# First expert of the first 448-column chunk in three passes; weights split by single parts in the experts' order; tokens split behind the ring

## The chip, the cores and the metric

The kernel runs on one core of a Trainium2 chip. The metric is device time in microseconds (us), less is better. The engines named below are TensorE (PE, with its weight loads as PEld), VectorE (DVE), ScalarE (ACT), GpSimd (POOL) and SyncE (SP, whose instruction stream issues most of the DMAs).

## The reference

Two stages run one after the other. The first is a linear attention with a polynomial sketch (4 batches, 4 heads, 1088 positions, head size 32, sketch size 8):

```python
a = einsum('rd,bhsd->bhsr', S1, x); b = einsum('rd,bhsd->bhsr', S2, x)   # for x = q and x = k
phi = outer product of a and b along r, 64 features
kv = sum over s of phi(k) v;  z = sum over s of phi(k)
out = (phi(q) kv) / (phi(q) z + 1e-6)
```

Its result, laid out as x[4352, 128], goes through four experts (E = 4, F = 1024) whose results are weighted with the normalised `domain_probs`:

```python
for e in range(4):
    h = maximum(x @ w1[e], 0)            # 4352 x 1024
    out += p[:, e:e+1] * (h @ w2[e])     # 4352 x 128
```

Everything is in float32.

## The kernel before

**Chunks and steps.** The 4352 tokens are cut into chunks of `CHUNKS = [128, 448, 512] + [448] * 7 + [128]` columns, numbered m = 0 to 10. In a chunk, each expert has eight tiles of 128 hidden rows, numbered k, and a step is two tiles. A chunk has NQ = 16 steps, four for each expert, so steps 0 to 15 are chunk 0, steps 16 to 31 chunk 1 (16 to 19 its expert 0, 20 to 23 expert 1, 24 to 27 expert 2, 28 to 31 expert 3), and step 32 opens chunk 2. A step stands in the program as half-steps, one for each tile. The program's order on each engine is fixed by the Python loop at the end; no engine reorders.

**Forms of a product.** Chunks 0 and 10 are "plain": products in float32 on half-width weights (L236). In the other chunks a first-layer tile is made in one of two ways. The float32 way is one product (`first`, L1111) and one Relu on ACT (L1113). The three-pass way (L1119 to L1129) works on numbers split into parts, tagged a, b and d, in the faster fp32r type: two products (L1124 with xa and wa, L1125 with xb and wb), a rescaling of the PSUM tile in place on ACT (L1126), a third product (L1173 with xd and wd) that is issued behind the next tile's first two, and then ACT's Relu: L1181 where the tile goes whole into the second layer, or L1176, followed by DVE's L1150 and L1153, where the hidden tile itself is split into ha, hb, hd. Before the change, expert 0 of chunk 1 takes the float32 way and all other experts of chunks 1 to 9 take three passes:

```python
def three_first(m, e):
    return not plain(m) and not (m == 1 and e == 0)
```

**The second layer.** In chunk 1 the experts 0 and 1 multiply whole hidden tiles in float32 (L1222). From expert 2 of chunk 1 on, six of an expert's eight tiles go through three passes in the order of `DEAL`, and the tiles 2 and 7 whole (all L1241). When an expert is finished, `gather` brings its PSUM bank out (`ev`, L1270 on ACT for a whole expert, L1244 on ACT and L1273 on DVE else), and POOL multiplies it with the gate and adds it to the chunk's total (L1280, L1282).

**The splits.** All weights and tokens are split on the fly, `split` on ACT (L896) and `join` on DVE (L899). A first-layer weight of an expert has six parts: a on ACT, b and d on DVE, for each half of its 1024 columns. The second-layer weights (`second_weight_parts`, two calls for an expert) take ACT 128x768, DVE 128x256 and 128x512 in the first call, and the same again in the second; the second ACT operation overwrites what the first pair of DVE joins reads, so it waits for them. `token_parts` makes xa on ACT, xb and then xd on DVE. The table `to_part` says behind which step each call stands: first-layer weights of the experts 1, 2, 3 and 0 from the steps 12, 13, 16 and 19 on, second-layer weights of the experts 2, 3, 0, 1 from the steps 16, 19, 22, 32 on, the tokens of chunk 1 behind the steps 17 and 18.

**Work beside it.** The attention of later tokens is cut into pieces (`plan`, `piece`, `work`) that are issued between the tiles: transposes kT (L387) and qT (L570), key projections (L430) with their ACT copies (L433) and DVE sums (L440), the copies of v into `vx` (`value_copy`, L396, L401), query projections (L236 from qT and sx, L761, then DMAs to `qd` and back), products (L782) and more. The columns of chunk 1 are written into the tile `ring` by small copies on DVE, POOL and ACT (L712) at about step 12. `gate_rows`, `store_gates` and `load_gates` compute and spread the gates by way of L330 on DVE, L331 on POOL, a transpose `pt` on DVE (L338) and DMAs of SP and POOL.

PSUM has six banks for tiles tagged h, which the first-layer tiles share with the pieces, and one each for o0 and o1.

Of the kernel before, what the change touches and what calls it, by code (L numbers as in the profile page):

```python
# [17 lines left out]
def _ap(t, p0: int, np_: int, off: int, free):  # L18

    p = list(t.ap)[0]  # L20
    return bass.AP(t.tensor, t.offset + p0 * p[0] + off, [[p[0], np_]] + [list(d) for d in free])
# [3 lines left out]
def kernel(  # L25
# [24 lines left out]
    nc = tc.nc  # L50
# [3 lines left out]
    B, H, S, D = q.shape  # L54
    E, DM, F = w1.shape
# [6 lines left out]
    NQ = E * FB // 2  # L62
# [13 lines left out]
        a6=10, b6=10, d5=11, d6=11, x7=11,  # L76
    )
    UNITS = [[P, 448, 512], [448, 448, 192], [256, 448, 384], [512, 320, 256]]

    CHUNKS = [P, 448, 512] + [448] * 7 + [P]  # L80
    NC = len(CHUNKS)
# [44 lines left out]
    kn, qn, vn = {}, {}, {}  # L126
# [10 lines left out]
    w1_of, w2_of = {}, {}  # L137
# [254 lines left out]
            nc.vector.transpose(kT[:, 1024:S], kn[b][:, 1024:S])  # L392

    def value_copy(b):
        for r in range(2):
            nc.scalar.copy(  # L396
                vx[:, 4 * r : 4 * r + 4, :, 0:D].rearrange("p t h d -> p h t d"),
                _ap(vn[b], 0, P, P * r, [[8 * D, H], [D, 4], [1, D]]),
            )
            yield  # L400
        nc.scalar.copy(vx[0:64, 8, :, 0:D], _ap(vn[b], 0, 64, 1024, [[D, H], [1, D]]))  # L401

    def key_project(b, gi, kf):

# [453 lines left out]
    def queries(b, c, n):  # L858
        qc = early.pop((b, c))
        qf = apool.tile([P, QW], F32, tag="qf", name="qf")  # L860
        nc.vector.stream_shuffle(in_=qc[:, 0:n], out=qf[:, 0:n], mask=mask_lo)
        yield
        nc.vector.tensor_tensor(out=qf[:, 0:n], in0=qc[:, 0:n], in1=qf[:, 0:n], op=ALU.add)
        free()
        yield
        qb = apool.tile([P, QW], F32, tag="qb", name="qb")
        nc.vector.stream_shuffle(in_=qf[:, 0:n], out=qb[:, 0:n], mask=mask_b)
        yield
        qp = query_tiles()
        for x in range(2):  # L870
            qa = apool.tile([P, QW], F32, tag="qa", name="qa")
            nc.vector.stream_shuffle(in_=qf[:, 0:n], out=qa[:, 0:n], mask=mask_a[x])  # L872
            yield
            for p in range(2):
                query_product(qp, p, x, n, qa, qb)
                yield
        yield
        yield
        yield
        yield from attend(b, c, n, qp)  # L880
# [10 lines left out]
    wa = cpool.tile([P, E, F], F32R, name="wa")  # L891
# [3 lines left out]
    def split(a, w, scale):  # L895
        nc.scalar.activation(a, w, ACTF.Copy, scale=scale * NEAR)  # L896

    def join(out, in0, scale, in1, op):
        nc.vector.scalar_tensor_tensor(out=out, in0=in0, scalar=scale, in1=in1, op0=ALU.mult, op1=op)  # L899

    def weight_parts(e):

        HF = F // 2
        for c in (slice(0, HF), slice(HF, F)):
            w, a, b, d = (x[:, c] for x in (w1_of[e], wa[:, e], wb[:, e], wd[:, e]))
            split(a, w, 4096.0)
            join(b, w, -4096.0, a.bitcast(F32), ALU.add)
            yield
            join(d, a.bitcast(F32), -R12, b.bitcast(F32), ALU.subtract)
            yield  # L910

    w2_parts = {}

    def second_weight_parts(e):


        w, n = w2_of[e, 0], N3 * DM
        vab = cpool.tile([P, F], F32R, tag=f"w1_{e}", name="vab")  # L920
        vb = cpool.tile([P, 2 * n - F], F32R, tag=f"vb_{e}", name="vb")
        a, lows = vab[:, 0:n], [(0, F - n, vab[:, n:F]), (F - n, n, vb[:, :])]
        split(a, w, 4096.0)
        for c, z, b in lows:
            join(b, w[:, c:z], 4096.0, a[:, c:z].bitcast(F32), ALU.subtract)
        yield
        split(a, w, 1.0)
        d = cpool.tile([P, n], F32R, tag=f"w2_{e}0", name="vd")[:, :]
        for c, z, b in lows:
            join(d[:, c:z], b.bitcast(F32), 1.0, a[:, c:z].bitcast(F32), ALU.subtract)  # L930
        w2_parts[e] = [
            tuple(x[:, DM * i - c : DM * i - c + DM] for x, c in ((a, 0), next((x, c) for c, z, x in lows if DM * i < z), (d, 0)))
            for i in range(N3)
        ]
        yield
# [114 lines left out]
    def plain(m):  # L1050
        return m in (0, NC - 1)
# [2 lines left out]
        return m == 1 and e < E // 2  # L1054

    def three_first(m, e):
        return not plain(m) and not (m == 1 and e == 0)

    begun_hp, made_hp = {}, {}

# [203 lines left out]
    def gather(m, e):  # L1264

        n = CHUNKS[m]
        o0, o1 = acc.pop((m, e))
        if o0 is None:
            ev = mpool.tile([P, CW], F32, tag="ev", bufs=1, name="ev")
            nc.scalar.copy(ev[:, 0:n], o1[:, 0:n])  # L1270
        else:
            ev = evs.pop((m, e))
            nc.vector.tensor_tensor(out=ev[:, 0:n], in0=ev[:, 0:n], in1=o1[:, 0:n], op=ALU.add)  # L1273
        g = gate.pop((m, e))[:, 0:n]
        if e == 0:
            total[m] = mpool.tile([P, CW], F32, tag="total", bufs=1, name="total")
        for c in range(0, n, 256):
            x = slice(c, min(c + 256, n))
            to = total[m] if e == 0 else ev
            nc.gpsimd.tensor_tensor(out=to[:, x], in0=ev[:, x], in1=g[:, x], op=ALU.mult)  # L1280
            if e:
                nc.gpsimd.tensor_tensor(out=total[m][:, x], in0=total[m][:, x], in1=ev[:, x], op=ALU.add)  # L1282
        yield
        later = m + (e + 2) // E
        if not plain(later):
            load_gates(later, [(e + 2) % E])
        if e == E - 1:
            yield
            yield

            for _ in range(0 if m + 2 < NC else 4):
                yield
            turn_back(m, total.pop(m)[:, 0:n])
# [40 lines left out]
        begun_hp[i] = psum(ps_h, "h")  # L1334
        half_columns(i, begun_hp[i], 0)
    to_part = {}
    for e, at, then in zip((1, 2, 3, 0), (12, 13, 16, 19), (32, 16, 19, 22)):
        for at, parts_of in ((at, weight_parts(e)), (then, second_weight_parts(e))):
            for step in range(at, at + 4):
                to_part.setdefault(step, []).append(parts_of)  # L1340
    for m in range(1, NC - 1):
        at, tokens = NQ * m - 4 if m > 1 else NQ + 1, token_parts(m)
        for step in (at, at + 1):
            to_part.setdefault(step, []).append(tokens)
    ending = iter(())

    def close(m, e):
# [40 lines left out]
    for i in range(len(steps) + LA):  # L1388
        if i < len(steps):
            m, kq = steps[i]  # L1390
            until_there(START[m] + CHUNKS[m])
            rate = max(
                [0]
                + [
                    (needed[c] - spent[0]) / max(sum(rooms[2 * i : 2 * NQ * c - (EARLY if c > 1 else 13)]), 0.3)
                    for c in range(m + 1, NC)
                    if 2 * NQ * c - (EARLY if c > 1 else 13) > 2 * i
                ]
            )

            def work():

                now[0] += 1
                if not NQ <= i < NQ + 2:
                    credit[0] = min(credit[0] + rate * rooms[min(now[0], len(rooms) - 1)], 0.5)
                if holds[0]:
                    credit[0] = max(credit[0], 0.01)
                while credit[0] > 0:
                    cost = piece()
                    credit[0] -= cost  # L1410
                    if not cost:
                        break

            first(i, work, lambda j: behind(2 * i + j))
            to_due(i)
            if kq == NQ - 4 and 0 < m < NC - 2:
                until_there(START[m + 1] + CHUNKS[m + 1])
            for parts_of in to_part.get(i, ()):
                next(parts_of, None)
            if i == 2:  # L1420
                gate_quotients()
            elif i == 8:
                later_weights()
            elif i == 5:
                load_batch(1)
            elif i == 12:
                gate_rows()
            elif i == 13:
                later_mask()
                store_gates(range(1))  # L1430
                load_gates(1, range(2))
            elif 14 <= i < 14 + B - 1:
                store_gates(range(i - 13, i - 12))
            if m == NC - 2 and kq == NQ // 2:
                until_there(B * S)
                load_last()
        if i == LA:

            made_hp[3] = psum(ps_h, "h")
            for c in (0, HP):  # L1440
                half_columns(3, made_hp[3], c)
        if NQ * (NC - 1) <= i < NQ * (NC - 1) + 2:
            continue
        if not behind(2 * i + 1):
            next(ending, None)
# [29 lines left out]
```

## Time and profile before

| | |
|---|---|
| median of 3 runs | 451.4 us (451.22 to 453.52) |
| the profiled execution's own time | 451.43 us |
| its span | 449.6 us, so 1.83 us lie around it |
| granted TensorE clock | 1.00 in all stretches that were looked at |
| PE, DVE, ACT, POOL busy | 443.5, 359.0, 330.6, 120.0 us |

Chunk 0 multiplies from about 14 to 33 us, and the eight float32 tiles of chunk 1's expert 0 start at 28.43 us. Chunk 2's first tile starts at 76.34 us. The busy time of PE includes waits inside its pipeline, because the ends of matmuls are modelled. The distance from the start of one matmul to the start of the next one that is not itself waiting is a better measure of what a matmul costs. A number in square brackets behind a row is idle time of that engine ahead of it, with what ended it.

### The profile page before, as it was taken

The numbers are of one execution on the slowest core, as the hardware profiler recorded it, in microseconds if no ns is written. First come the engines' busy times: TensorE is split into PE (matmuls) and PEld (weight loads), VectorE is DVE, ScalarE is ACT, GpSimd is POOL, SyncE is SP. The second block draws the span as 40 slices with busy tenths as digits, with TensorE's granted clock in tenths as the row PEclk, the third lists the DMA queues.
The fourth block names the chain that finished last, engine by engine and source line by source line (L and its number), as shares of the span: only waits on it lengthen the run. The fifth ranks groups of instructions, "written<-read, shape, count | busy, mean of one in ns | idle before, by whom it ended". The sixth has DMA issues, their size and how long they took to land.

```text
span 449.6 us, 8655 instructions
## 1 busy us (share of the span) xinstructions
PE 443.5 (99%) x3013; PEld 367.4 (82%) x3013; DVE 359.0 (80%) x606; ACT 330.6 (74%) x699; POOL 120.0 (27%) x206
## 2 busy tenths in 40 slices
PE   8999999999999999999999999999999999999997
PEld 5875678777778888888888888888888888888886
DVE  5887779887988896889879869787779787787753
ACT  4268888677867876778687767787788788877741
POOL 7352133210323132212322312134123212321320
PEclk9999999999999999999999999999999999999999
DMA  7964641014223403242252142410321121117401
GB/s 200 298 143 142 189 129 49 26 33 124 94 55 91 120 23 80 52 128 68 68 127 24 22 117 72 123 47 21 95 53 30 30 46 40 22 37 219 154 2 28
DMA packets 53779, 38.45 MB, mean 86 GB/s; under 512 B 26920, under 2 KB 49896, under 8 KB 53736
## 3 DMA queue, kind: packets, MB, share of 16 engines
q1 hardware_dynamic: 53064, 37.77, 31.9%
q8 instruction: 23, 0.38, 0.3%
q0 software_dynamic: 448, 0.07, 0.2%
q14 instruction: 20, 0.16, 0.1%
q10 hardware_dynamic: 224, 0.07, 0.1%
HBM read 32.68 MB, written 5.21 MB: 84 GB/s over the span
## 4 chain that ended last, share of the span: by engine, by line
PE 94%; DVE 3%; DMA 1%; ACT 1%; issue 0%; SPq 0%; DVEq 0%
PE o L1241 40%; PE h L1173 13%; PE h L1124 13%; PE h L1125 13%; PE h L236 7%; PE o L236 3%; PE o L1222 2%; PE h L1111 1%; PE h L430 1%; DMA kn<-in_k_dram 1%; DVE qp L583 1%; DMA vn<-in_v_dram 0%; ACT h L1126 0%; DVE qa L872 0%; DVE rd L615 0%
## 5 line engine op out<-in xcount | busy, mean ns | idle before, releaser
L1126 ACT ACTIVATE h<-h 128x448 f32<-128x448 f32 (+1 forms) x280 | 151.3, 540 | 74.0 <-PE h L1125 69.5
L1150 DVE SCALAR_TENSOR_TENSOR hb<-h,ha 128x448 fp32r<-128x448 f32 (+1 forms) x204 | 125.9, 624 | 54.5 <-ACT ha L1176 53.2
L1124 PE MATMUL h<-xa,wa 128*128 128x448 f32 (+1 forms) x280 | 130.3, 465 | 0.0
L1153 DVE SCALAR_TENSOR_TENSOR hd<-ha,hb 128x896 fp32r<-128x896 f32 (+1 forms) x102 | 116.7, 1144 | 8.2
L1176 ACT ACTIVATE ha<-h 128x448 fp32r<-128x448 f32 (+1 forms) x204 | 111.7, 548 | 0.0
L1173 PE MATMUL h<-xd,wd 128*128 128x448 f32 (+1 forms) x280 | 103.5, 370 | 0.5 <-ACT h L1126 0.4
L1125 PE MATMUL h<-xb,wb 128*128 128x448 f32 (+1 forms) x280 | 103.1, 368 | 0.0
L1280 POOL TENSOR_TENSOR ev<-ev,gate 128x256 f32<-128x256 f32 (+1 forms) x54 | 40.9, 757 | 219.4 <-DVE ev L1273 201.7
L1241 PE MATMUL o<-ha,vab 128*128 128x448 f32 (+1 forms) x204 | 76.3, 374 | 0.0
L1125 PEld LDWEIGHTS h<-xb,wb 128*128 128x128 f32 x280 | 52.7, 188 | 18.8 <-issue 14.8
L1124 PEld LDWEIGHTS h<-xa,wa 128*128 128x128 f32 x280 | 52.7, 188 | 18.7 <-issue 13.5
L1241 PE MATMUL o<-hid,w_sb 128*128 128x448 f32 (+1 forms) x136 | 62.9, 544 | 0.0
L1173 PEld LDWEIGHTS h<-xd,wd 128*128 128x128 f32 x280 | 52.5, 187 | 9.2 <-ACT h L1126 2.6
L1241 PE MATMUL o<-hd,vd 128*128 128x448 f32 (+1 forms) x204 | 58.9, 370 | 0.0
L1241 PE MATMUL o<-hb,vb 128*128 128x448 f32 (+1 forms) x136 | 49.9, 368 | 0.0
L1282 POOL TENSOR_TENSOR total<-total,ev 128x256 f32<-128x256 f32 (+1 forms) x54 | 46.1, 853 | 4.2
L1181 ACT ACTIVATE hid<-h 128x448 f32<-128x448 f32 (+1 forms) x76 | 42.1, 554 | 0.1
L1241 PEld LDWEIGHTS o<-ha,vab 128*128 128x128 f32 x204 | 38.3, 188 | 4.2 <-issue 0.2
L1241 PEld LDWEIGHTS o<-hd,vd 128*128 128x128 f32 x204 | 38.1, 188 | 3.6
L1280 POOL TENSOR_TENSOR total<-ev,gate 128x256 f32<-128x256 f32 (+1 forms) x18 | 12.7, 726 | 78.0 <-issue 57.4
L1241 PEld LDWEIGHTS o<-hid,w_sb 128*128 128x128 f32 x136 | 25.6, 188 | 2.2
L1241 PEld LDWEIGHTS o<-hb,vb 128*128 128x128 f32 x136 | 25.5, 188 | 1.9
(142 smaller groups left out, 450.5 us busy)
## 6 DMA issues: line engine op xcount, KB each, us to landing
gate<-gates SPq DMA_DIRECT2D x24, 224.0 KB
kn<-in_k_dram SPq DMA_DIRECT2D x4, 544.0 KB
vn<-in_v_dram SPq DMA_DIRECT2D x16, 128.0 KB
w_last<-in_moe_w_dram SPq DMA_DIRECT2D x4, 512.0 KB
w_sb<-in_moe_w_dram SPq DMA_DIRECT2D x3, 512.0 KB
w_sb<-in_moe_w_dram SPq DMA_DIRECT2D x6, 256.0 KB
qp<-qd SPq DMA_DIRECT2D x6, 224.0 KB
qb<-qd SPq DMA_DIRECT2D x6, 224.0 KB
```

The lines of the kernel that those rows point to most:

```text
L236: nc.tensor.matmul(out(s), weights(s), moving(s), **flags)
L1124: nc.tensor.matmul(g, wa[:, e, w], xa, start=True, stop=False)
L1125: nc.tensor.matmul(g, wb[:, e, w], xb, start=False, stop=True)
L1126: nc.scalar.activation(g, g, ACTF.Copy, scale=1.0 + R12)
L1150: nc.vector.scalar_tensor_tensor(out=hb, in0=g, scalar=0.0, in1=high, op0=ALU.max, op1=ALU.subtract)
L1153: nc.vector.scalar_tensor_tensor(out=d2, in0=a2.bitcast(F32), scalar=R12, in1=b2.bitcast(F32), op0=ALU.mult, op1=ALU.subtract)
L1173: nc.tensor.matmul(g, w, x, start=False, stop=True, skip_group_check=True)
L1176: nc.scalar.activation(ha, g, ACTF.Relu, scale=NEAR)
L1181: nc.scalar.activation(hid[i][j], g, ACTF.Relu)
L1241: nc.tensor.matmul(acc[m, e][o][:, 0:n], w, h, start=first_one, stop=last)
L1280: nc.gpsimd.tensor_tensor(out=to[:, x], in0=ev[:, x], in1=g[:, x], op=ALU.mult)
L1282: nc.gpsimd.tensor_tensor(out=total[m][:, x], in0=total[m][:, x], in1=ev[:, x], op=ALU.add)
```

## The change

Expert 0 of chunk 1 takes three passes in the first layer as well; its second layer stays whole. Its weights and the tokens of chunk 1 are therefore split before step 16. The first-layer weights are now split by single parts with a table, `SPLITS`, of part, expert, half and step (one part, b of expert 0's first half, stands inside `queries` behind its last product instead). The second-layer weights of the experts 0 and 1 are split later than before (behind the steps 31 and 32, and 35 and 36), those of 2 and 3 behind 18, 19 and 21, 22. The copies of v for batch 1 go from ACT to POOL, and the `ev` copy of a whole expert goes from ACT to DVE.

```diff
+    SPLITS = [
+        ("a", 0, 0, 4), ("a", 0, 1, 5), ("a", 1, 0, 6), ("a", 1, 1, 7), ("a", 2, 0, 9), ("d", 0, 0, 11),
+        ("b", 0, 1, 12), ("d", 0, 1, 13), ("a", 2, 1, 13), ("b", 1, 0, 14), ("d", 1, 0, 15), ("a", 3, 0, 15),
+        ("b", 1, 1, 16), ("d", 1, 1, 17), ("b", 2, 0, 16), ("d", 2, 0, 17), ("b", 2, 1, 17), ("d", 2, 1, 18),
+        ("a", 3, 1, 17), ("b", 3, 0, 19), ("d", 3, 0, 19), ("b", 3, 1, 20), ("d", 3, 1, 20),
+    ]
+    W2_AT = (18, 19), (21, 22), (31, 32), (35, 36)
+    TOKENS_AT = 11, 12
...
     def value_copy(b):
+        copy = nc.gpsimd.tensor_copy if b == 1 else nc.scalar.copy
         for r in range(2):
-            nc.scalar.copy(
+            copy(
...
         for x in range(2):
...
             for p in range(2):
                 query_product(qp, p, x, n, qa, qb)
                 yield
+        weight_part("b", 0, 0)
         yield
...
-    def weight_parts(e):
-
-        HF = F // 2
-        for c in (slice(0, HF), slice(HF, F)):
-            w, a, b, d = (x[:, c] for x in (w1_of[e], wa[:, e], wb[:, e], wd[:, e]))
+    def weight_part(what, e, h):
+
+        c = slice(F // 2 * h, F // 2 * (h + 1))
+        w, a, b, d = (x[:, c] for x in (w1_of[e], wa[:, e], wb[:, e], wd[:, e]))
+        if what == "a":
             split(a, w, 4096.0)
+        elif what == "b":
             join(b, w, -4096.0, a.bitcast(F32), ALU.add)
-            yield
+        else:
             join(d, a.bitcast(F32), -R12, b.bitcast(F32), ALU.subtract)
-            yield
...
     def three_first(m, e):
-        return not plain(m) and not (m == 1 and e == 0)
+        return not plain(m)
...
         if o0 is None:
             ev = mpool.tile([P, CW], F32, tag="ev", bufs=1, name="ev")
-            nc.scalar.copy(ev[:, 0:n], o1[:, 0:n])
+            nc.vector.tensor_copy(ev[:, 0:n], o1[:, 0:n])
...
-    for e, at, then in zip((1, 2, 3, 0), (12, 13, 16, 19), (32, 16, 19, 22)):
-        for at, parts_of in ((at, weight_parts(e)), (then, second_weight_parts(e))):
-            for step in range(at, at + 4):
-                to_part.setdefault(step, []).append(parts_of)
-    for m in range(1, NC - 1):
-        at, tokens = NQ * m - 4 if m > 1 else NQ + 1, token_parts(m)
-        for step in (at, at + 1):
-            to_part.setdefault(step, []).append(tokens)
+    for what, e, h, step in SPLITS:
+        at_step(step, lambda p=(what, e, h): weight_part(*p))
+    for e, at in zip((2, 3, 0, 1), W2_AT):
+        parts_of = second_weight_parts(e)
+        for step in at:
+            at_step(step, next_of(parts_of))
+    for m in range(2, NC - 1):
+        tokens = token_parts(m)
+        for step in (NQ * m - 4, NQ * m - 3):
+            at_step(step, next_of(tokens))
+    tokens = token_parts(1)
+    for step in TOKENS_AT:
+        at_step(step, next_of(tokens))
```

`at_step` appends a call to the list of a step, and `next_of` makes the call that advances a generator once.

More of the change, by code (lines that the diff above doesn't have):

```diff
@@ L400, in value_copy @@
             yield
-        nc.scalar.copy(vx[0:64, 8, :, 0:D], _ap(vn[b], 0, 64, 1024, [[D, H], [1, D]]))
+        copy(vx[0:64, 8, :, 0:D], _ap(vn[b], 0, 64, 1024, [[D, H], [1, D]]))
     def key_project(b, gi, kf):
@@ L1336, with at_step, next_of @@
     to_part = {}
-    for e, at, then in zip((1, 2, 3, 0), (12, 13, 16, 19), (32, 16, 19, 22)):
-        for at, parts_of in ((at, weight_parts(e)), (then, second_weight_parts(e))):
-            for step in range(at, at + 4):
-                to_part.setdefault(step, []).append(parts_of)
-    for m in range(1, NC - 1):
-        at, tokens = NQ * m - 4 if m > 1 else NQ + 1, token_parts(m)
-        for step in (at, at + 1):
-            to_part.setdefault(step, []).append(tokens)
+    def at_step(step, *calls):
+        to_part.setdefault(step, []).extend(calls)
+    def next_of(parts_of):
+        return lambda: next(parts_of, None)
+    for what, e, h, step in SPLITS:
[11 more added lines that the diff above has]
+        at_step(step, next_of(tokens))
     ending = iter(())
@@ L1417 @@
                 until_there(START[m + 1] + CHUNKS[m + 1])
-            for parts_of in to_part.get(i, ()):
-                next(parts_of, None)
+            for part in to_part.get(i, ()):
+                part()
             if i == 2:
```

## The prediction

> **What bounds the kernel now.** I read the page first, then the chain that ended last, the stretches around the change, and the timeline from 15 to 100 us row by row.
>
> ```profile
> PE 443.5 (99%) x3013; PEld 367.4 (82%) x3013; DVE 359.0 (80%) x606; ACT 330.6 (74%) x699; POOL 120.0 (27%) x206
> PE 94%; DVE 3%; DMA 1%; ACT 1%; issue 0%; SPq 0%; DVEq 0%
> ```
>
> TensorE carries the chain, so a change counts by the PE time that it takes out and by the waits that it puts into PE. The price of the products is read in expert 1 of chunk 1, where three passes and a float32 product alternate:
>
> ```profile
> 46.38 0.37 PE L1173 MATMUL h<-xd,wd 128*128 128x448 f32 x1
> 46.59 0.91 PE L1222 MATMUL o<-hid,w_sb 128*128 128x448 f32 x2
> 46.99 0.71 PE L1124 MATMUL h<-xa,wa 128*128 128x448 f32 x1
> 47.54 0.36 PE L1125 MATMUL h<-xb,wb 128*128 128x448 f32 x1
> 47.74 0.37 PE L1173 MATMUL h<-xd,wd 128*128 128x448 f32 x1
> ```
>
> One tile is 47.74 - 46.38 = 1.36 us. Back-to-back fp32r passes start 0.20 apart (46.18, 46.38, 46.59), so three are 0.61 and the float32 product the other 0.75. That is the core of the change: 0.75 becomes 0.61, eight times.
>
> The stretch that is rewritten opens so:
>
> ```profile
> 28.43 1.77 PE L1111 MATMUL h<-ring,w_sb 128*128 128x448 f32 x4
> 30.13 0.66 PE L236 MATMUL o<-w_sb,hid 128*64 128x128 f32 x8
> 30.72 1.77 PE L1111 MATMUL h<-ring,w_sb 128*128 128x448 f32 x4
> 32.42 1.08 PE L236 MATMUL h<-qT,sx 128*64 128x256 f32 x8
> 33.34 0.61 PE L236 MATMUL o<-w_sb,hid 128*64 128x128 f32 x8
> 33.87 1.02 PE L1222 MATMUL o<-hid,w_sb 128*128 128x448 f32 x2
> ...
> 44.91 0.47 PE L1173 MATMUL h<-xd,wd 128*128 128x448 f32 x1 [0.40 <-ACT h L1126]
> ```
>
> Four float32 tiles take 5.44 us to 33.87, and the first third pass of expert 1 waits for ACT, which is late behind splits and copies. The engines to which second-layer splits are moved look like this:
>
> ```profile
> 50.00:60.00 10.00, 10.00 (x72) 7.09 (x70) 5.99 (x14) 7.42 (x16) 0.00 (x0) 1.00 0.65 165
> 70.00:80.00 10.00, 10.00 (x46) 8.41 (x46) 9.76 (x14) 8.46 (x18) 4.14 (x4) 1.00 0.09 28
> ```
>
> After the stretch's length the columns are PE, PEld, DVE, ACT and POOL busy, then clock and DMA. DVE is at 60% from 50 to 60 us and at 98% from 70 to 80.
>
> **The opening, steps 16 to 19.** I lay the new order out by hand with those rows. ACT's L1126 starts 0.04 behind the modelled end of a second pass (0.36 row) and lasts 0.53; the next ACT operation follows 0.47 later; a third pass starts 0.06 behind L1126. From 28.43: passes to 29.44, third pass waiting to 29.84 (0.40 lost), the plain product 0.44, two passes, second third pass 30.89, two passes, third pass waiting to 31.68 (0.18 lost), the query projection 0.87, plain 0.44. The first L1222 starts at 33.19 instead of 33.87: gain 0.68. From there to the fifth L1222 before takes 42.02 - 33.87 = 8.15. After, it is four tiles of three passes (2.45), four float32 products (3.00) and nine key projections (2.03), 7.49: the fifth starts at 40.68, gain 1.34. Then two more tiles at 1.36 bring the seventh to 43.40, against 45.22: gain 1.82, in which the wait at 44.91 is gone. Over all eight tiles the passes alone give 8 x 0.14 = 1.1; the rest is that wait and the exposed starts of the float32 groups (28.43 to 30.13 is 1.70 for 1.50).
>
> ACT has to cover this: eight tiles of 1.0 (L1126 and L1181), `qs` 0.37, wa 0.63, three `fs` 0.95, two vab 1.7, together 11.7, in PE's 12.6. It fits because three `vx` copies (1.54) leave for POOL, two `ev` copies (1.07) for DVE, and wa's leave for chunk 0. If it did not, each ACT microsecond over would be a PE one.
>
> **The parts moved into chunk 0.** Five wa splits of 0.63 fall in the gaps between Relus of 0.38 at 0.87 spacing (0.49 idle). Four in a row delay the Relus by at most 0.18 to 0.56; PE reads one about 1.3 us later: nothing. wb of the first half stands on DVE where it waits 0.67 for PE (21.21 to 21.88): nothing. xa is put ahead of a Relu on ACT and waits for the `ring` copies of DVE (end 25.93) and POOL (25.87). It ends at 26.58, so that Relu ends at 26.93 instead of 26.20; PE needs it at 27.02. Cover of 0.09; without it each 0.1 is PE's. On DVE, wd, xb, wb and xd (0.65 each) come ahead of L330. xb ends at 27.26 (first pass at 28.43), xd at 28.46 (third pass 29.84). Behind them L330, then POOL's L331, `pt` (30.0 to 30.3 instead of 29.32), SP's four and POOL's twelve gate stores, two gate loads and the load of q are late by about 1. They sit ahead of `qd` on SP: it goes out at 34.65 instead of 35.39, since `qs` is early. By the same delays the last factor lands at 50.5 and DVE's second L782 ends at 51.2; PE needs it at about 51.5: nothing, or 0.4 if the queue gives no lead. The second kT transposes end at 38.06 for a projection at 38.2: nothing, up to 0.4 if DVE slips.
>
> **POOL copies.** No POOL copy of 128x512 is in the trace. The nearest rows are 0.30 for 32x128 (L712) and 0.84 to 0.87 for a two-input 128x256 (L1282); ACT needs 0.62. I take 1.2 each, between 0.6 and 1.7, 3 us in all, behind the gate stores from about 38. Only the key sums at 84.35 read them: nothing directly. DVE pays for overlap:
>
> ```profile
> 27.78 0.63 DVE L899 SCALAR_TENSOR_TENSOR wd<-wa,wb 128x512 fp32r<-128x512 f32 x1
> 28.02 0.67 POOL L331 TENSOR_TENSOR pn<-dp,dsum 128x136 f32<-128x136 f32 x1 [2.15 <-DVE dsum L330]
> 28.32 0.91 DVE L899 SCALAR_TENSOR_TENSOR wb<-w_sb,wa 128x512 fp32r<-128x512 f32 x1
> ```
>
> The join that meets a POOL operation takes 0.91 instead of 0.63. The Trainium skill, "SBUF — State Buffer", section "Who interferes with whom", makes this an exclusive lock: a VectorE operation with two SBUF inputs blocks against a GpSimd one that reads SBUF, for the whole instruction, and which loses depends on who started first. The trace agrees in sign, 0.28 lost here. By that rule the copies could hold up DVE for their whole length. From the rows, I take two losses of 0.28, 0.5 of DVE time, hidden, against the copies' own 3 us as the other end (a rival).
>
> **ev on DVE.** Two copies of about 0.61 (L1273's 448-column row). The second stands behind hd at 62.2 and must free o1 before 63.48: it does, and the ACT wait at 61.53 shrinks by 0.08. DVE is then 0.6 later up to about 78.
>
> **Second-layer splits of experts 0 and 1.** Expert 0's (ACT 2 x 0.85, DVE 2 x 1.10) leave 52 to 58 us, where they held up no PE, and go behind the steps 31 and 32; expert 1's leave 79 to 85 for the steps 35 and 36. What happens shows in the old place:
>
> ```profile
> 52.64 0.84 ACT L896 ACTIVATE vab<-w_sb 128x768 fp32r<-128x768 f32 x1 [0.99 <-DVE wb L899]
> ...
> 79.05 0.85 ACT L896 ACTIVATE vab<-w_sb 128x768 fp32r<-128x768 f32 x1
> ...
> 80.43 0.19 PEld L1173 LDWEIGHTS h<-xd,wd 128*128 128x128 f32 x1 [0.42 <-ACT h L1126]
> ```
>
> An ACT split may wait for DVE, and the L1126 behind it then holds PE's third pass. On the old clock: the first vab comes at 76.86, L1126 of chunk 2's first tile moves from 77.05 to 77.6, its third pass from 77.88 to 78.24. DVE, busy to 78.92, makes the two joins by 80.0. The second vab waits for them from 79.62, and the L1126 behind it moves from 79.78 to 80.73: third pass 81.37 instead of 80.43. **Loss 0.94**, or 1.54 if DVE still carries the 0.6 of ev. PE's key sums (84.35 to 86.6) then let ACT (3.15 idle) and DVE (1.61 idle) catch up.
>
> At steps 35 and 36 the first vab (90.66) moves one L1126 from 90.78 to 91.4: 0.31. DVE is at hd and qT until 93.43, so its joins end at 94.4, the second vab starts at 94.46, and L1126 of the tile behind it at 95.2 instead of 93.33. Its third pass moves from 94.29 to 95.84: **loss 1.55** with the 0.31 in it. If DVE gets there earlier, only 0.3 remains.
>
> **The sum.** 451.43 (the profiled execution, which is also the median) - 1.82 - 0.08 + 0.94 + 1.55 = 452.0. The measurement tells about 0.5%, 2.3 us, from no change.
>
> **The rivals.**
> - *A, as summed: 452.0.* For it: the ACT waits on DVE joins and 98% DVE at 70 to 80 us. Chance 0.45.
> - *B, the split waits are absorbed: 449.5.* The opening's 1.9 stays, with 0.0 to 0.3 lost later. For it: PE has second-layer work to do in between, and ACT is only 85% busy. Against: a third pass lost 0.4 at 80.43 already. Below 449.1 needs more than the 1.9 that I can find. Chance 0.27.
> - *C, slower: 454.1.* The chain join, vab, L1126, third pass at steps 31 to 36 with DVE later by ev's 0.6: 1.54 there, 0.6 more at step 36 (2.15), and only the 1.1 of the passes gained: 451.43 - 1.1 + 1.54 + 2.15 = 454.0, and 0.1 from the Relu behind xa. It decides where DVE is over 0.6 late at 78 us. Chance 0.14.
> - *D, POOL's copies block DVE in 38 to 42 us.* Up to 3 us of DVE, of which the sums that free PSUM banks (due at 42.75, expected at 40.2) pass on 0.5: 452.5. For it: the 0.28 above and 1.62 for L1153 at 61.17 beside POOL, against 1.09. Chance 0.08. The lock that the Trainium skill states would be this case at its full length.
> - *E, three passes are no cheaper here:* ACT, at 11.7 of 12.6, bounds expert 0, the 1.9 is lost and the late waits stay: 453.9. Chance 0.06.
>
> **Range and chances.** 449.4 to 454.1 takes in A with its bounds, most of B, D, E and C's middle. A's own range is 450.8 to 453.0. Faster by over 0.5%: a third of B and a little of A, 0.11. Slower by over 0.5%: two thirds of C, over half of E and tails of A, 0.15. Within: 0.74.
>
> **What would show it.** The first L1222 near 33.2 and expert 1's seventh float32 product near 43.4 show the gain; L1126 waits on PEld of 0.3 to 0.6 in steps 16 and 17 the price. Chunk 2's first tile should start near 74.4 and the key sums near 83.4. Idle time ahead of vab on ACT with DVE as releaser, and PEld waits for L1126 around 80 and 94 us, show the losses; none there means B. Wrong altogether would be PE waiting for xd, kT or a PSUM bank before 45 us.

## The result and the profile after

The changed kernel takes **454.48 us** (median of 6 runs, 454.17 to 456.26) against 451.54 (6 runs, 451.22 to 453.52) for the kernel before: a ratio of **1.0067 [1.0043, 1.0091]**, 2.9 us slower. The profiled execution took 454.17 us with a span of 452.3, so 1.9 us lie around the span where before had 1.8: the loss is inside. The forecast of 452.0 was on the right side of no change by 0.6 us, but 2.5 us too low, and the time lies above the top of the range. The forecast had called a slowdown of over 0.5% unlikely, with a chance of 0.15.

Line numbers of the changed kernel are 9 to 11 higher: L1126 is L1135, L1173 is L1182, L1222 is L1231, L1241 is L1250, L896 is L907, L899 is L910. (In the experiments that move the load of q, lines behind the new ones are 2 higher still.) The line of its page that answers to the one of before, the chain that ended last:

```profile
PE 93%; DVE 5%; ACT 1%; issue 1%; DVEq 0%; ACTq 0%
```

DVE has taken 2 points of the chain and DMA has left it. Where that happens is found by setting each matmul of the one trace beside the same matmul of the other. The start after minus the start before, at places on the old clock:

| old clock, us | what is there | after minus before, us |
|---|---|---|
| 33.87 | first L1222 | -0.05 |
| 42.02 | fifth L1222 | -0.65 |
| 45.63 to 55.2 | expert 1 | -1.14 to -1.02 |
| 69.92 | third pass behind the split of xa | -0.21 |
| 76.34 | chunk 2's first tile | -0.16 |
| 80.43 | third pass behind the second vab of expert 0 | +0.66 |
| 91.73 | behind the first vab of expert 1 | +0.97 |
| 94.29 | behind the second vab of expert 1 | +2.19 |
| 445.94 | last matmul | +2.62 |

So there is a gain of 1.1 us up to 45 us, of which 0.2 is given back near 55 us and 0.75 at one wait at 70 us (-0.96 just ahead of it, -0.21 behind), and then the loss at the steps 31 to 36.

**The opening.** TensorE's timeline of the changed kernel from 28 to 34 us:

```profile
29.69 0.47 PE L1182 MATMUL h<-xd,wd 128*128 128x448 f32 x1 [0.21 <-ACT h L1135]
30.09 0.66 PE L245 MATMUL o<-w_sb,hid 128*64 128x128 f32 x8
30.68 0.48 PE L1133 MATMUL h<-xa,wa 128*128 128x448 f32 x1
...
31.97 0.47 PE L1182 MATMUL h<-xd,wd 128*128 128x448 f32 x1
32.37 1.08 PE L245 MATMUL h<-qT,sx 128*64 128x256 f32 x8
33.28 0.61 PE L245 MATMUL o<-w_sb,hid 128*64 128x128 f32 x8
33.82 1.02 PE L1231 MATMUL o<-hid,w_sb 128*128 128x448 f32 x2
```

The plain product takes 30.68 - 30.09 = 0.59 where the forecast laid out 0.44, and what follows the third passes at 29.69 and 31.97 starts 0.40 later instead of 0.20. The stretch takes 33.82 - 28.40 = 5.42 us; with four float32 tiles it took 5.44. But these 5.42 us hold only eleven of the twelve passes: three L1182 stand in them, and that of the fourth tile comes behind the first L1231, for another 0.20. So these four tiles cost about 0.2 us more in three passes than in float32.

**The wait at 70 us.** ACT's timeline from 57 to 70.5 us, then TensorE's from 69 us, of the changed kernel:

```profile
68.59 0.63 ACT L907 ACTIVATE xa<-ring 128x512 fp32r<-128x512 f32 x1 [0.69 <-DMA ring<-xd]
69.13 0.53 ACT L1135 ACTIVATE h<-h 128x448 f32<-128x448 f32 x1
```

```profile
69.71 0.47 PE L1182 MATMUL h<-xd,wd 128*128 128x448 f32 x1 [0.60 <-ACT h L1135]
```

Before, ACT's split of chunk 2's tokens did not wait (ACT's timeline of before from 66 to 70 us):

```profile
68.73 0.63 ACT L896 ACTIVATE xa<-ring 128x512 fp32r<-128x512 f32 x1
```

Now ACT arrives 0.8 earlier, but the DMA that fills `ring` does not, and the rescaling behind the split (L1135) holds the third pass. Why the DMA stood still is read from SP's timeline, from 28 to 78 us:

```profile
34.15 0.38 SPq L118 DMA_DIRECT2D qn<-in_q_dram  x1
34.62 1.16 SPq L773 DMA_DIRECT2D qd<-qs  x2
40.61 0.60 SPq L778 DMA_DIRECT2D qp<-qd  x1
...
65.84 0.34 SPq L737 DMA_DIRECT2D ring<-xd  x1
```

In before the load of q stands at 33.58, `ring` at 65.42, and between them:

```profile
35.39 1.16 SPq L763 DMA_DIRECT2D qd<-qs  x2
40.52 0.60 SPq L768 DMA_DIRECT2D qp<-qd  x1
```

The stores of `qd` are issued 0.77 earlier, as forecast (34.65), but the loads that wait for them go out no earlier: the 544 KB load of q ahead of them on the same queue is issued 0.57 later. From there on the products, the attention's result, `xd` and `ring` keep their old times within 0.5 us. The 0.2 us near 55 us belongs to the same chain: DVE waits 2.27 us for the last factor up to 51.16, two joins of a second-layer split stand behind it on DVE, ACT's vab waits 2.37 for these, and the third pass at 54.21 waits for the rescaling behind vab.

**The second-layer splits.** ACT's timeline of the changed kernel from 70 to 99 us, at the two places that the forecast priced:

```profile
79.71 0.85 ACT L907 ACTIVATE vab<-w_sb 128x768 fp32r<-128x768 f32 x1 [0.27 <-DVE vb L910]
...
95.10 0.84 ACT L907 ACTIVATE vab<-w_sb 128x768 fp32r<-128x768 f32 x1 [0.93 <-DVE vb L910]
95.85 0.58 ACT L1135 ACTIVATE h<-h 128x512 f32<-128x512 f32 x1
```

DVE's and TensorE's rows at the second of them:

```profile
93.40 0.70 DVE L580 STREAM_TRANSPOSE qT<-qn 128x256 f32<-128x256 f32 x2
94.02 0.38 DVE L910 SCALAR_TENSOR_TENSOR vab<-w_sb,vab 128x256 fp32r<-128x256 f32 x1
94.33 0.68 DVE L910 SCALAR_TENSOR_TENSOR vb<-w_sb,vab 128x512 fp32r<-128x512 f32 x1
```

```profile
96.48 0.50 PE L1182 MATMUL h<-xd,wd 128*128 128x512 f32 x1 [0.95 <-ACT h L1135]
```

DVE makes the two joins only after `hd` and `qT`. The second vab overwrites what the joins read, the rescaling stands behind it on ACT, and the third pass waits for that. All waits of TensorE's weight loads for that rescaling, from 60 to 100 us, are in this line (us in total, times, longest); in before it was 1.0, 3, 0.5:

```profile
PEld h L1182 <- ACT h L1135: 4.8, 6, 1.4
```

### The profile page after: what moved, and what is told of

The parts are those of the page before. It is cut to its first block, busy times and chain, and to the rows that moved or that the text cites. A ratio compares the mean times of both kernels' runs of the same rounds, so it can differ in the third digit from the quotient of the medians.

```text
span 452.3 us, 8673 instructions
## 1 busy us (share of the span) xinstructions
PE 445.3 (98%) x3021; PEld 369.1 (82%) x3021; DVE 358.7 (79%) x608; ACT 332.5 (74%) x702; POOL 120.8 (27%) x209
## 4 chain that ended last, share of the span: by engine, by line
PE 93%; DVE 5%; ACT 1%; issue 1%; DVEq 0%; ACTq 0%
PE o L1250 38%; PE h L1182 13%; PE h L1133 13%; PE h L1134 12%; PE h L245 9%; PE o L245 3%; PE o L1231 3%; PE h L440 1%; PE h L233 1%; DVE hd L1162 1%; DVE hb L1159 1%; ACT h L1135 1%; DVE qp L593 0%; DVE qa L882 0%; DVE vb L910 0%
## 5 line engine op out<-in xcount | busy, mean ns | idle before, releaser
L1135 ACT ACTIVATE h<-h 128x448 f32<-128x448 f32 (+1 forms) x288 | 155.4, 540 | 78.0 <-PE h L1134 73.2
L1133 PE MATMUL h<-xa,wa 128*128 128x448 f32 (+1 forms) x288 | 134.9, 468 | 0.0
L1182 PE MATMUL h<-xd,wd 128*128 128x448 f32 (+1 forms) x288 | 107.4, 373 | 2.5 <-ACT h L1135 2.1
L1134 PE MATMUL h<-xb,wb 128*128 128x448 f32 (+1 forms) x288 | 105.9, 368 | 0.0
L1250 PE MATMUL o<-ha,vab 128*128 128x448 f32 (+1 forms) x204 | 76.4, 374 | 0.0
L1133 PEld LDWEIGHTS h<-xa,wa 128*128 128x128 f32 x288 | 54.2, 188 | 19.8 <-issue 14.6
L1134 PEld LDWEIGHTS h<-xb,wb 128*128 128x128 f32 x288 | 54.2, 188 | 19.5 <-issue 15.5
L1182 PEld LDWEIGHTS h<-xd,wd 128*128 128x128 f32 x288 | 54.0, 187 | 13.8 <-ACT h L1135 7.1
L1250 PE MATMUL o<-hid,w_sb 128*128 128x448 f32 (+1 forms) x136 | 63.0, 544 | 0.0
L1250 PE MATMUL o<-hd,vd 128*128 128x448 f32 (+1 forms) x204 | 58.8, 369 | 0.0
L1250 PE MATMUL o<-hb,vb 128*128 128x448 f32 (+1 forms) x136 | 49.9, 368 | 0.0
L1190 ACT ACTIVATE hid<-h 128x448 f32<-128x448 f32 (+1 forms) x84 | 46.4, 552 | 0.2
L1250 PEld LDWEIGHTS o<-ha,vab 128*128 128x128 f32 x204 | 38.3, 188 | 4.2 <-issue 0.2
L1250 PEld LDWEIGHTS o<-hd,vd 128*128 128x128 f32 x204 | 38.1, 188 | 3.4
L1250 PEld LDWEIGHTS o<-hid,w_sb 128*128 128x128 f32 x136 | 25.6, 188 | 2.3
L1250 PEld LDWEIGHTS o<-hb,vb 128*128 128x128 f32 x136 | 25.5, 188 | 1.9
```

What stands on the lines that cost most here:

```text
L1133: nc.tensor.matmul(g, wa[:, e, w], xa, start=True, stop=False)
L1134: nc.tensor.matmul(g, wb[:, e, w], xb, start=False, stop=True)
L1135: nc.scalar.activation(g, g, ACTF.Copy, scale=1.0 + R12)
L1182: nc.tensor.matmul(g, w, x, start=False, stop=True, skip_group_check=True)
L1190: nc.scalar.activation(hid[i][j], g, ACTF.Relu)
L1250: nc.tensor.matmul(acc[m, e][o][:, 0:n], w, h, start=first_one, stop=last)
```

## The experiments

**The theories.** *W*: the loss is the later second-layer splits, by joins that ACT waits for, and it is about the forecast's 2.5 us whatever the first expert does. *R*: the gain of the opening is real, and is given back at the wait for `ring`, since the query chain through DMA did not move. Against them stood that three passes are no cheaper than float32 here (rival E), and that the copy of `ev` or POOL's copies make DVE late (rivals C and D). All medians stand beside runs of the kernel before on the same chip (451.47, 451.54 and 451.59 in the three groups); "end" is the shift of the last matmul against before in the profiled execution. Medians and ends can differ, because what lies behind the start of the last matmul, such as the landing of the last store, varies from execution to execution: 5.5 us in before, 6.8 in e9, 7.2 in e10. The end leaves that out, but it is the reading of one execution. Each of these also has a shift of its own from the first matmuls at 14 us on, before any edit can act. Read at 27.89 it is -0.28 in e2, -0.19 in e9, -0.17 in e4, -0.14 in e3, -0.11 in e5, +0.11 in e14, +0.18 in e11, and at most 0.06 in the others. Shifts are given as read; where two runs are set beside one another, this first one is taken off ("from its own start").

**e1: the later splits alone.** The kernel before, with the second-layer splits of the experts 0 and 1 on late steps:

```diff
-    for e, at, then in zip((1, 2, 3, 0), (12, 13, 16, 19), (32, 16, 19, 22)):
+    for e, at, then in zip((1, 2, 3, 0), (12, 13, 16, 19), (35, 16, 19, 31)):
```

> The kernel before with one edit: the second-layer splits of experts 0 and 1 go behind the steps 31, 32 and 35, 36. Theory W (the place of these splits costs PE time by itself, because ACT's second split waits for DVE's joins and holds up a rescaling and so a third pass): about 2.2 us slower than before, 453.7, with PE waits for ACT near 80 and 94 us. Rival G (they cost only where the rest of the change has run PE ahead of the other engines): within 0.5 us of before.

Measured: 454.01 us (453.77 to 454.36), ratio 1.0057 [1.0045, 1.0069]; +0.84 at 80.43, +1.15 at 91.73, +2.37 at 94.29, end +2.59. ACT's waits from 60 to 100 us in it:

```profile
ACT vab L896 <- DVE vb L899: 1.3, 2, 0.9
```

This single edit costs nearly as much as the whole change, and the changed kernel's line for the same wait says 1.2, 2, 0.9. `ev` and the copies of v stay on ACT in e1, so neither move is needed for the loss.

**e2 and e3: the splits elsewhere.** The changed kernel with the second layer's table altered. e2 puts them early, e3 leaves a step between the two calls of an expert:

```diff
-    W2_AT = (18, 19), (21, 22), (31, 32), (35, 36)
+    W2_AT = (18, 19), (21, 22), (23, 24), (32, 33)   # e2
+    W2_AT = (18, 19), (21, 22), (31, 33), (35, 37)   # e3
```

> The changed kernel with these splits at the steps 23, 24 and 32, 33 instead. Theory W: 1.9 to 2.3 us less than the changed kernel, 452.2 to 452.6, about 0.7 to 1.0 over before by the drift behind 97 us, or even with before if that drift is a consequence. The gain of the passes stays eaten by the wait for the ring near 69.7 us. Rival G': the loss sits elsewhere, 454.0 to 454.5.

> The changed kernel with two steps between the calls: 31, 33 and 35, 37. If the wait of ACT's second split for DVE's joins (0.27 and 0.93 us idle in the trace) is the price, about 1.2 us less, 453.3, and no idle time ahead of vab near 80 and 95 us. If the price is the work that is put on ACT and DVE in these steps, 454.2 to 454.7, as the changed kernel.

e2 measured 452.09 us (451.33 to 453.59), ratio 1.0017 [1.0007, 1.0027]: 2.4 less than the changed kernel. The loss behind 70 us is gone, but its offsets, -1.39 at 45.63, go to -0.98 at 53.96, -0.45 at 55.43, -0.19 at 63.88 and +0.82 at 69.92, and the end is +1.04 (the traced execution is one of its two longest, 453.55 us). DVE's timeline from 46 us and ACT's from 68 us in e2 show where:

```profile
51.62 0.69 DVE L792 TENSOR_TENSOR qp<-qp,qb 128x512 f32<-128x512 f32 x1 [2.81 <-DMA qb<-qd]
```

```profile
69.62 0.63 ACT L907 ACTIVATE xa<-ring 128x512 fp32r<-128x512 f32 x1 [0.95 <-DMA ring<-xd]
```

Both are the query chain: the last factor at 51.6, which the second half of the products waits for and behind which the joins of a split are late once more, and 18 us later the `ring`. The step at 63.88 is another thing: there TensorE waits 0.4 us for DVE's copy of `ev`, which with the early splits comes later on DVE (62.5 against 61.3 us in the changed kernel).

e3 measured 453.63 us (452.63 to 454.77), ratio 1.0049 [1.0032, 1.0065], end +1.86. ACT no longer waits for joins, and from 69.92 on it loses 1.4 instead of 2.8. Of what is left, 0.65 (0.42 at 82.63 and 0.23 at 96.54) is a new wait, of TensorE for the late parts themselves; most of the rest is the rescaling behind the first vab of each expert. The new wait in the waits from 60 to 100 us:

```profile
PEld o L1250 <- ACT vab L907: 1.0, 2, 0.6
```

**e4 and e5: the tokens of chunk 2 split later.** e4 is the changed kernel with this edit, e5 has e2's table too:

```diff
-        for step in (NQ * m - 4, NQ * m - 3):
+        for step in (NQ * m - 3, NQ * m - 2) if m == 2 else (NQ * m - 4, NQ * m - 3):
```

> The changed kernel with the token split of chunk 2 one step later (29 and 30 instead of 28 and 29), so that ACT does not stand waiting for the ring's DMA. Theory D (this in-order wait took 0.8 of the gain at 69.7 us): 453.7, 0.8 less. Rival (ACT was late in any case): 454.5, or later still since xd comes closer to its use in step 32.

> The changed kernel with the second-layer splits at 23, 24 and 32, 33 and the token split of chunk 2 at 29 and 30. If the ring wait is the rest of the loss, ACT no longer stands at it and about 0.8 of the passes' gain comes through: 451.2, at most 0.3 under before. If the wait only moves (xa and xd late for step 32), 452.1, as with the early splits alone.

e4 measured 454.74 us (453.98 to 456.3), ratio 1.0074 [1.0058, 1.009]: no gain, which the expectation missed. The wait at 70 us is gone (-0.93 still at 73 us), but the lead is lost at the next place: +0.76 at 80.43 and end +2.57. ACT's timeline at 79 us:

```profile
79.81 0.84 ACT L907 ACTIVATE vab<-w_sb 128x768 fp32r<-128x768 f32 x1 [1.14 <-DVE vb L910]
```

The second vab comes at 79.81 against 79.71, though ACT was ready 0.77 earlier: DVE sets this time here, and TensorE's lead is worth nothing at it. (The edit also puts the joins xb and xd a step later on DVE, so this is no test of the lead alone.) The two losses are therefore not added up: here the later one swallows what the earlier one had left. e5, with early splits, measured 452.01 us (451.0 to 452.95), ratio 1.0008 [0.9998, 1.0018], end +0.22. Its lead, -1.22 at 45.63, shrinks to -0.83 at 53.96, where the products wait for the last factor, to -0.30 at 55.43, by the late joins, and to -0.05 at 63.88, mostly by the copy of `ev`. So putting off the one reader of `ring` is not enough.

**e9, e10 and e11: the chain itself.** e9 is e2 with the load of q for batch 1 moved behind the two stores of `qd`; e10 has e4's edit too; e11 is the kernel before with the load moved, and is the control.

```diff
-        if u == len(UNITS[b]) - 1 and b + 1 < B:
+        if u == len(UNITS[b]) - 1 and 0 < b < B - 1:
             load_rows(q, b + 1, "qn")
...
             nc.sync.dma_start(qd[b, u, :, n2 * s : n2 * s + n2], qs[half[s], 0:n2])
+        if b == 0:
+            load_rows(q, 1, "qn")
```

> The changed kernel with the second-layer splits at 23, 24 and 32, 33, and SP's load of the second batch's q put behind the two stores of the first query unit instead of ahead of them. Theory Q: those stores queue behind that 544 KB load, so the query factors, the visit, y and the ring of chunk 2 come at the same time however early PE is. Then the stores land near 38 us instead of 40.3, the wait of DVE for the last factor near 51 us and of ACT for the ring near 69.6 go, and the time is 450.4 to 451.0. Rival: the chain is bound by its own store, load and issue times; 452.1.

> As the run before it, with the token split of chunk 2 at 29 and 30 as well. Under theory Q nothing more is to be had: within 0.4 us of that run. If the ring is still late there, 0.3 to 0.8 less than that run.

> The control: the kernel before with only the move of the q load. Before has no wait for the ring and 1.8 us of DVE idle time for the last factor that no PE work waits for, so under theory Q it stays within 0.5 us of before. If it gains as much as the changed kernel does, the move is worth something by itself and says nothing of the change.

SP's timeline of e9:

```profile
34.00 1.16 SPq L773 DMA_DIRECT2D qd<-qs  x2
35.21 0.58 SPq L118 DMA_DIRECT2D qn<-in_q_dram  x1
38.07 0.60 SPq L780 DMA_DIRECT2D qp<-qd  x1
...
64.41 0.34 SPq L737 DMA_DIRECT2D ring<-xd  x1
```

From the issue of `qd` to the load that waits for it are 38.07 - 34.00 = 4.07 us with the q load behind, 5.95 in e2 (34.37 to 40.32) with it ahead. `ring` follows at 64.41, 1.4 before the changed kernel's and 2.4 before e2's. ACT's split of xa, at 67.69, no longer waits, and the offsets stay: -1.30 at 45.63, -1.04 at 67.87, end **-0.88** (-0.69 from its own start). The median is 451.39 us (450.41 to 452.43), ratio 0.9995 [0.9985, 1.0005], between the 450.4 to 451.0 of theory Q and the 452.1 of its rival: the chain moved as expected, and the total gained less. e10 measured 451.11 us (450.7 to 452.58), 0.9993 [0.9984, 1.0001], end -0.51. In e11 the chain moves as well (`qp` load 38.42 for 40.52, `ring` 64.35 for 65.42), yet it measured 451.48 us (451.23 to 451.72), 0.9997 [0.9988, 1.0006], end +0.25 (+0.07 from its own start): the earlier chain is worth nothing by itself, only as cover for the earlier TensorE.

**e6 and e12: what the three passes bring.** e2 and e9 with expert 0 back in float32, its splits left where the change puts them:

```diff
-        return not plain(m)
+        return not plain(m) and not (m == 1 and e == 0)
```

> The changed kernel with the second-layer splits at 23, 24 and 32, 33, and expert 0 of chunk 1 back in float32; all other edits stay. Prices the three passes where the DMA chain is as it was. If that chain sets when chunk 2's tokens can be split, the passes bring nothing here: 451.3 to 452.2, level with the three-pass form (452.1). If the passes' 1.1 us come through in part, 452.6 to 453.2.

> The same float32 form with the q load behind the two stores, to be set against the three-pass form with that load (451.4, last PE operation 0.88 us ahead of before). With the chain out of the way the passes should be worth their 0.9 to 1.2 us of PE: last PE operation level with before within 0.3, time 451.5 to 452.3.

e6 measured 452.47 us (451.79 to 453.08), 1.0015 [1.0006, 1.0023], between the two ranges that were expected, end +0.59; e2's three passes gave 452.09, 1.0017 and +1.04. The ratios are level. In the traces, from its own start, e6 has a lead of 0.60 at 44.91 against 0.99, and at 69.92 it stands at +0.19 against +1.10. With the chain unmoved, the lead of the passes brought nothing that lasts.

e12 measured 451.42 us (451.23 to 451.56), 0.9995 [0.9986, 1.0004], end -0.22. Beside e9's 451.39 and 0.9995 the medians are level, so no total shows a gain of the passes, and the 0.9 to 1.2 that were expected did not come. In the traces, from its own start, e9 is ahead of e12 by 0.40 us at 45.63 (1.11 against 0.71) and by 0.51 at the last matmul (0.69 against 0.18). So of the 1.1 us that the opening gains, 0.4 are the passes'. The other 0.7 come with expert 0 in float32 as well, 0.67 of them at one third pass, which in before waits for ACT at 44.91 and here does not (TensorE's timeline of e12 from 43 to 45.5 us):

```profile
44.28 0.36 PE L1184 MATMUL h<-xd,wd 128*128 128x448 f32 x1
```

The first four tiles give nothing: e12 comes to its first L1233 at 33.83, the changed kernel, with three passes, at 33.82.

**e13 and e14: toward a better version.** e13 is e9 with `ev` back on ACT and a step between the split calls; e14 is e9 with the copies of v back on ACT.

```diff
+    W2_AT = (18, 19), (21, 22), (22, 24), (32, 34)   # e13
+            nc.scalar.copy(ev[:, 0:n], o1[:, 0:n])   # e13
+        copy = nc.scalar.copy                        # e14
```

> A candidate: three passes, the q load behind the stores, the ev copies back on ACT, second-layer splits at 22, 24 and 32, 34. It takes away the one PE wait for ev on DVE (0.5 on PEld) and ACT's waits for joins: last PE operation 1.1 to 1.4 us ahead of before, time 450.3 to 451.0. If ACT is too full for ev, level with the three-pass form with the q load, 451.4.

> The three-pass form with the q load behind the stores, and the v copies of batch 1 on ACT as before. If POOL's copies cost DVE time that reaches PE (rival D of the prediction), up to 0.5 less; if they relieve ACT in steps 20 to 24, 0.3 to 0.8 more, with PE waits for ACT near 40 us; else within 0.3 of 451.4.

e13 measured 451.05 us (450.54 to 451.91), ratio **0.9986 [0.9976, 0.9996]**, end -0.66; e14 451.01 (450.69 to 453.0), 0.9990 [0.9981, 0.9998], end -0.34. Both are ahead of the kernel before by an interval that excludes 1, and of the changed kernel by over 3 us, but 0.1% is all that the rewritten opening brings when nothing takes it back. e13's last matmul is not the 1.1 to 1.4 ahead that were expected; it is level with e9's (0.66 against 0.69 from its own start). What `ev` and the copies of v are worth singly stays open: the two medians are 0.04 apart. Of `ev` the trace shows that TensorE waits 0.5 us for DVE's copy in e9 and in e14 (in the line for L1252, released by DVE's `ev`), which takes 0.34 of e9's lead near 63.5 us, and not in e13, which loses 0.18 to a rescaling at 61.53 instead. Of the copies of v, e14's median is 0.4 under e9's, which its expectation took as the sign that POOL's copies cost something; the traces say the opposite, a lead of 0.86 at 45.63 against 1.11 from its own start, because a third pass waits for ACT again.

## Why the prediction was wrong

**Right: steps 31 to 36.** This was the largest term, 0.94 + 1.55 = 2.49. The offset goes from -0.21 at 69.92 to +2.19 at 94.29, 2.40 us, by the mechanism named: DVE's joins behind `hd` and `qT`, ACT's second vab behind them, L1135, third pass. Singly: -0.16 to +0.66 is 0.82 for 0.94; 0.31 at 91.73 for 0.31; and +0.66 to +2.19 is 1.53 for 1.55. That the first size is so close is in part luck: it was laid out on the old clock, and the lead was gone when TensorE came there. With a lead of 0.93 left, in e4, the same place took 1.69. e1 puts a price of 2.4 to 2.6 on it with nothing else changed. Rival B, that these waits are absorbed, fell.

**Wrong in size: the opening.** 1.82 was forecast at the seventh product, 45.22 - 44.09 = 1.13 came. Of the 0.69 that is missing, 0.63 lies ahead of the first L1222, at 33.82 for 33.19. The layout charged 0.44 for a plain product and 0.20 from each third pass to what follows. The rows say 0.59 and 0.54, and 0.40 twice. The 0.59 and 0.53 of before stood in the rows that the prediction shows (30.13 to 30.72, 33.34 to 33.87). The step that failed is "Over all eight tiles the passes alone give 8 x 0.14 = 1.1", with "the exposed starts of the float32 groups" as a gain on top: the groups of plain products begin and end with such a start too, and the three-pass order keeps these. Instead of 1.1 the passes gave 0.4 (e12): about 0.2 lost in the first four tiles, 0.15 gained in each of the other four. The 0.72 beside them came, as 0.7, nearly all of it at the wait at 44.91. The rest of the layout held: first to fifth L1222 7.55 (7.49 forecast), fifth to seventh 2.72 as laid out, and no wait at 44.91.

**Missing: what is queued behind a DMA.** The text followed `qd` to its issue at 34.65 (34.62 came) and asked only about the last factor. It did not follow that chain to its end, `xd` and `ring`, nor ask whether ACT's split of chunk 2's tokens at 68.73 would still find `ring` written when ACT came a microsecond or more earlier. That cover was thin, and it was priced at nothing by not being listed. This took the offset from -1.14 to -0.21, 0.93 us, of which 0.75 at the wait for `ring`; e9 keeps most of the lead by moving the load, and e11 shows that the move alone gives nothing. The issue of `qd` was a wrong proxy: its landing is what counted, and that depends on the 544 KB ahead of it: 5.95 us from issue to the waiting load in e2 and 4.07 in e9, 5.13 in before and 2.86 in e11. The Trainium skill, "DMA: Bandwidth & Descriptors", section "Queues, rings and completion order", puts the DMAs that SP issues on one row of rings, and on each DMA engine the descriptors are consumed in ring order; the 5.95 and 4.07 us of e2 and e9 agree with it.

**The sum.** -1.14 at the seventh tile, +0.93 given back by 70 us, +2.40 from there to 94 us, +0.43 in the rest of the kernel: +2.62 at the last matmul, against the forecast's +0.59. Of the 2.03 between the two, the opening makes 0.69, the query chain 0.93 and the rest of the kernel 0.43; the splits came out 0.09 less, and the 0.08 that the forecast took off apart for a shorter wait of ACT, of which 0.04 came at 61.53, is in the chain's figure. Of the last 0.43, 0.11 stands right behind the wait at 94.29 (+2.30 at 94.52), as in e1; the other 0.32 comes in small steps up to 350 us, which no wait near the change explains. The control e11 drifts by 0.1 there as well (+0.17 at 94.29, +0.27 at 225), so a part of it belongs to the execution and not to the edit. The losses also do not stack, as e4 shows: where DVE sets the time of the second vab, a larger gain of the opening would have been lost as well, which is argued from e4 and was not run by itself. The forecast netted a gain on TensorE against losses whose times DVE sets.

**The rivals.** C had the right sign and nearly the time (454.1 for 454.5), but not the cause, so that its time is near is luck: its point was DVE being over 0.6 late by `ev`, and in the changed kernel the row of `hb` at 76.34 is earlier than the one of before at 76.58. `ev` is not needed, by e1; where it does cost TensorE something is at 63.5 us, with the early splits (e2, e5, e9). E (453.9) had the right sense of the first four tiles and not of all eight. D did not come: POOL's two large copies took 0.63 each, not 1.2, and TensorE waited for no bank. The join beside them, DVE's and POOL's timelines at 37 us:

```profile
36.88 0.87 DVE L910 SCALAR_TENSOR_TENSOR wd<-wa,wb 128x512 fp32r<-128x512 f32 x1
```

```profile
37.52 1.26 POOL L406 COPY vx<-vn 128x512 f32<-128x512 f32 x2
```

It took 0.87 for the usual 0.65 to 0.69, a loss of about 0.2, near the 0.28 taken. But the two overlap for only 0.23 us (37.52 to 37.75): DVE then waits for ACT until 38.88, when the large copies are over. So no run here shows what a copy costs DVE that runs beside it for its whole length. None of the signs for "wrong altogether" appeared: TensorE waited for neither xd, nor kT, nor a PSUM bank before 45 us. The sign that did decide, the key sums at 85.02 where 83.4 was forecast, was written down as a test of the gain.

## What to carry to other kernels

When work on the critical engine moves forward, follow every transfer whose reader moves with it to the end of its chain, and list the cover that is left at each reader: a lead of 1 us was lost at two in-order waits whose releaser stayed (DVE for the last factor, then a split on ACT for `ring`). Price the landing of a DMA and not its issue, with what is ahead of it on its queue. A split that must wait for another engine's joins costs the critical engine all that is queued behind it, so it belongs where that other engine is idle (a step between its halves only traded half of the loss for a later part); and losses whose time is set by another engine can swallow earlier gains (e4), so they are not simply to be netted against them. Before two traces are compared by the shift of their matmuls, take off the shift that they have before the edit.

## What the runs showed that was not expected

- The order of three DMAs on SP's queue moved the landing of two 64 KB stores by 1.9 us (5.95 in e2 to 4.07 in e9 from issue to the load that waits for them), and `ring`, 26 us later, from 66.79 to 64.41.
- Where groups of plain products stand between them, four tiles of three passes took about 0.2 us more than four of float32 (5.42 with one pass still to come, against 5.44). With passes in an unbroken row, a tile is about 0.15 us cheaper.
- A GpSimd copy of 128x512 took 0.63 us, as long as the same copy on ACT (0.62), where a gate product of 128x256 on GpSimd takes 0.84.
